# Moving weight conversion and erf, and adding idle-time products, in the first batch of a fused attention and feed-forward kernel

## Chip, cores and metric

The kernel runs on one core of one Trainium2 chip. The metric is the device time of one execution in microseconds (us). Every time below is a median over several executions of one build, all of them fast (one core, runs of one kernel within 1% of each other, with a mean granted clock of 0.976 or more; the granted clock is the share of TensorE's full clock that the profile shows). Times of single instructions come from one profiled execution of each kernel.

## The reference

Attention in both directions between a sequence `x` and a small `state`, and behind it a feed-forward block on all 4352 rows:

```python
B, H, S, Ns, D = 8, 8, 512, 32, 64          # d_model = H*D = 512, d_ff = 2048
scores  = scale * x @ state^T;  a  = softmax(scores);   xread = a  @ state     # (B,H,S,D)
scores2 = scale * state @ x^T;  a2 = softmax(scores2);  sread = a2 @ x         # (B,H,Ns,D)
rows = concat([xread, sread], axis=2)  ->  (B*(S+Ns), 512)                     # shortened
h  = rows @ w_in                       # 512 x 2048
g  = h * erf(softplus(h))
out = g @ w_out                        # 2048 x 512
```

`w_in` and `w_out` arrive as 64-bit floats. The kernel turns them into 32-bit floats itself, in eight pieces each.

## The kernel before

`xread @ w_in` is done as `a @ (state @ w_in)`: the code calls the inner product the *mixed* matrix (`m`), and each of the four *groups* of hidden columns of the first batch needs its own. A group g is: the mixed matrix, four hidden tiles (two products each, summed in one bank of PSUM, then *evicted*, that is read out of it, by ScalarE's softplus and VectorE's copy), erf and product, then 16 products with `w_out` (`project`). The mixed matrix of group g needs w_in pieces 2g and 2g+1; `project` of group g needs w_out pieces 2g and 2g+1. All of this shares three `raw` buffers for fetched pieces.

```python
def weight(dst, src, shape):
    ...
    raw = act.tile([P, 2 * shape[0] * i], U32, name="raw", bufs=3)
    fetched.append(nc.sync.dma_start(out=raw..., in_=src.bitcast(U32)))
    ...
    nc.scalar.activation(out=dst, in_=hi.bitcast(F32), func=ACTF.Copy, scale=2.0 ** -112)     # L111
    nc.scalar.activation(out=lo, in_=lo, func=ACTF.Copy, scale=2.0 ** -29)                     # L112
    nc.vector.tensor_scalar(d, d, 3, None, op0=ALU.logical_shift_left)                        # L113
    nc.vector.tensor_tensor(d, d, lo, op=ALU.add)                                             # L114
    nc.vector.scalar_tensor_tensor(out=d, in0=hi, scalar=0x80000000, in1=d, ...)              # L115
...
def warm(n):                      # idle-time products, for TensorE's clock (e1, e9)
    for _ in range(n):
        nc.tensor.matmul(out=spare[:, 0:P], lhsT=ident, rhs=ident, start=True, stop=True)
...
def hidden(b, fts, t0, n):
    ...
    for i in range(4):
        ...                                                        # products into hp
        banks.append((nc.scalar.activation(out=s[:, i, :], in_=hp, func=ACTF.Softplus),
                      nc.vector.tensor_copy(hs[:, i, :], hp)))
    nc.scalar.activation(out=s, in_=s, func=ACTF.Erf)
    return s, hs, nc.vector.tensor_tensor(s, s, hs, op=ALU.mult), banks
...
def weights(g, banks):            # first batch, after hidden() of group g
    if g + 1 < NG:
        for j in range(2):
            on_act, on_dve = banks[2 * j + 1]
            with tc.issue_after(on_act.ins), tc.issue_after(on_dve.ins):
                weights_in(2 * g + 2 + j)
        on_act, on_dve = mixed(0, g + 1)
    else:
        on_act, on_dve = banks[3]
    with tc.issue_after(on_act.ins), tc.issue_after(on_dve.ins):
        weights_out(g)
...
    before, gT = gT, first()      # first() is hidden(), before is the group ahead
    if b == 0:
        weights(g, gT[3])
    if b == 0 and g == 3:
        with tc.issue_after(before[2].ins):
            rest()                # the state's attention of batch 0: exp, transposes, a2T, sT
    if pending is not None:
        pending()                 # project() of the group ahead
```

`issue_after(x)` puts the next instructions behind `x` in the order of the program. That order is fixed when the kernel is built, by an estimate of when each instruction is ready.

## Time and profile before

| what | before |
|---|---|
| time, median (range) of 3 runs | 818.99 us (818.62 to 820.32) |
| span of the profiled run | 819.1 us |
| TensorE busy | 97% |
| mixed matrix of group 1 starts | 45.91 us |
| group 2 / group 3 starts (first hidden product) | 73.69 / 96.31 us |
| `project` of group 2 ends | 120.86 us |
| attention transposes of batch 2 start | 131.69 us |

A line of the timeline gives start, duration, engine, source line, operation, output<-inputs, shapes and how many records were joined; in brackets is the idle time before it and what ended that. A product of the hidden tiles or with w_out is two records, each 0.43 us at a granted clock of 1.00 and 0.86 us at 0.50, from start to start (the text calls the two full clock and half clock). The prediction shows the page's main rows, the chain through the large hole and the clock windows; these lines of TensorE's timeline before complete them. They show group 3 without a hole of note: the products with w_out of group 2 start at 101.38 and flow on among small work.

```profile
96.31 3.70 PE L273 MATMUL h<-aT,m 128*128 128x512 f32 x8
...
101.38 1.98 PE L283 MATMUL o<-w_out,s 128*128 128x512 f32 x4 [0.82 <-DVE w_out L115]
...
111.32 9.61 PE L283 MATMUL o<-w_out,s 128*128 128x512 f32 x22
```

### The profile page before, as it was taken

Reading aid. Unit: us, or ns where it says so; the run is one execution under the profiler, and the core shown is the slowest. Engines: PE = TensorE matmul, PEld = TensorE weight load, DVE = VectorE, ACT = ScalarE, POOL = GpSimd, SP = SyncE. Lnnn points to the kernel's source line nnn. Section 1 sums busy time; section 2 is a strip of 40 time slices with the busy share of each in tenths; the row PEclk is TensorE's granted clock in tenths of the full one; section 3 lists DMA queues with packets and bytes.
Section 4 is the critical chain, followed back from the end, with each engine's and each line's share of the span. In section 5 each row is a group of like instructions: output and inputs, shape, how many; then the busy total and the mean of one; then the engine's idle time right before and its main releaser. Section 6 shows DMA issues by size and latency. Waiting matters only on the chain.

```text
span 819.1 us, 10493 instructions
## 1 busy us (share of the span) xinstructions
PE 791.8 (97%) x4460; PEld 605.8 (74%) x4460; DVE 429.0 (52%) x626; ACT 369.4 (45%) x465; POOL 0.7 (0%) x6
## 2 busy tenths in 40 slices
PE   7779999999999999999999999999999999999997
PEld 5223344678888788878888788878887888888886
DVE  3577785457445554547453744555454745353431
ACT  5557754637333733345343733363334533333320
POOL 0000000000000000000000000000000000000000
PEclk9769999999999999999999999999999999999999
DMA  6354730201100020002000020000000000000000
GB/s 209 129 179 149 234 103 26 79 0 25 54 0 27 1 78 0 27 1 78 0 26 1 16 63 1 26 1 26 1 27 1 27 1 26 1 26 1 26 1 26
DMA packets 47414, 35.27 MB, mean 43 GB/s; under 512 B 36872, under 2 KB 36872, under 8 KB 47368
## 3 DMA queue, kind: packets, MB, share of 16 engines
q1 hardware_dynamic: 45256, 34.09, 13.4%
q10 hardware_dynamic: 2112, 0.52, 0.3%
q8 instruction: 35, 0.57, 0.3%
q14 instruction: 11, 0.09, 0.0%
HBM read 25.69 MB, written 8.91 MB: 42 GB/s over the span
## 4 chain that ended last, share of the span: by engine, by line
PE 89%; ACT 5%; DVE 3%; issue 2%; DMA 1%; SPq 0%; DVEq 0%
PE o L335 44%; PE h L273 30%; PE at L256 4%; PE o L283 4%; PE at L157 1%; PE at L198 1%; PE at L180 1%; PE at L227 1%; PE at L215 1%; ACT s L277 1%; ACT L275 1%; ACT L277 1%; DMA x<-in_x_dram 1%; DVE w_in L114 1%; ACT s L275 1%
## 5 line engine op out<-in xcount | busy, mean ns | idle before, releaser
L273 PE MATMUL h<-aT,m 128*128 128x256 f32 (+1 forms) x960 | 245.4, 403 | 1.0 <-ACT m L258 0.7
L273 PEld LDWEIGHTS h<-aT,m 128*128 128x128 f32 x960 | 179.1, 192 | 66.6 <-issue 35.6
L276 DVE COPY hs<-h 128x512 f32<-128x512 f32 x136 | 93.4, 689 | 187.6 <-ACT s L275 187.6
L275 ACT ACTIVATE s<-h 128x512 f32<-128x512 f32 x136 | 80.4, 597 | 166.9 <-PE h L273 166.6
L278 DVE TENSOR_TENSOR s<-s,hs 128x2048 f32<-128x2048 f32 x34 | 77.9, 2292 | 80.1 <-ACT s L277 80.1
L335 PE MATMUL o<-w_out,s 128*128 128x256 f32 x480 | 114.9, 380 | 1.6 <-DVE s L278 1.6
L335 PE MATMUL o<-raw,hs 128*128 128x256 f32 x480 | 115.5, 380 | 0.0
L335 PE MATMUL o<-w_out,hs 128*128 128x256 f32 x480 | 113.4, 379 | 0.0
L335 PEld LDWEIGHTS o<-w_out,s 128*128 128x128 f32 x480 | 90.2, 190 | 14.3 <-DVE s L278 2.5
L335 PEld LDWEIGHTS o<-w_out,hs 128*128 128x128 f32 x480 | 91.1, 190 | 12.3
L335 PEld LDWEIGHTS o<-raw,hs 128*128 128x128 f32 x480 | 90.3, 190 | 12.4
L258 ACT COPY m<-at 128x512 f32<-128x512 f32 (+1 forms) x33 | 18.9, 573 | 163.4 <-PE at L256 163.4
L277 ACT ACTIVATE s<-s 128x2048 f32<-128x2048 f32 x34 | 64.9, 1910 | 0.4
L283 PE MATMUL o<-w_out,s 128*128 128x512 f32 x128 | 59.2, 602 | 1.3 <-DVE w_out L115 1.3
L335 PE MATMUL o<-raw,s 128*128 128x256 f32 x240 | 56.7, 379 | 0.0
L275 ACT ACT_TABLE_LOAD x40 | 51.3, 1283 | 0.7
L258 DVE COPY m<-at 128x512 f32<-128x512 f32 (+1 forms) x33 | 22.2, 674 | 54.9 <-PE at L256 54.9
L256 PE MATMUL at<-w_in,stT 64*32 64x512 f32 (+1 forms) x528 | 40.1, 609 | 10.6 <-DVE w_in L115 10.1
L335 PEld LDWEIGHTS o<-raw,s 128*128 128x128 f32 x240 | 45.2, 190 | 5.9
L283 PEld LDWEIGHTS o<-w_out,s 128*128 128x128 f32 x128 | 23.0, 190 | 32.3 <-issue 29.7
L277 ACT ACT_TABLE_LOAD x34 | 43.6, 1283 | 0.6
L346 ACT COPY m<-o 128x256 f32<-128x256 f32 x15 | 5.6, 372 | 57.3 <-PE o L335 57.3
(71 smaller groups left out, 569.2 us busy)
## 6 DMA issues: line engine op xcount, KB each, us to landing
raw<-in_moe_w_in_dram SPq DMA_DIRECT2D x8, 1024.0 KB, 5.7
raw<-in_moe_w_out_dram SPq DMA_DIRECT2D x8, 1024.0 KB, 4.8
out_dram<-ot SPq DMA_DIRECT2D x32, 256.0 KB, 2.4
x<-in_x_dram SPq DMA_DIRECT2D x60, 128.0 KB, 2.8
x<-in_x_dram ACTq DMA_DIRECT2D x4, 128.0 KB, 4.0
out_dram<-ot SPq DMA_DIRECT2D x8, 64.0 KB, 1.7
st<-in_state_dram SPq DMA_DIRECT2D x8, 56.0 KB, 4.1
st<-in_state_dram SPq DMA_DIRECT2D x2, 32.0 KB
```

Of the source, the lines that this page charges most:

```text
L114: nc.vector.tensor_tensor(d, d, lo, op=ALU.add)
L157: nc.tensor.transpose(out=xp[:, P * c:P * c + P], in_=xt[:, c, 2 * i:2 * i + 2, :], identity=ident)
L180: on_pe = nc.tensor.transpose(out=s1[:, NI * c:NI * c + NI, :], in_=sc[:, e, P * c:P * c + P], identity=ident)
L256: nc.tensor.matmul(out=ps[e][q, :], lhsT=stT[b][r, q], rhs=w_in[r, fs, i, :], start=True, stop=True)
L258: return nc.scalar.copy(mg[:, 0], ps[0]), nc.vector.tensor_copy(mg[:, 1], ps[1])
L273: nc.tensor.matmul(out=hp[:, n * j:n * j + n], lhsT=lhsT, rhs=rhs, start=(k == 0), stop=(k == len(ops) - 1))
L275: banks.append((nc.scalar.activation(out=s[:, i, :], in_=hp, func=ACTF.Softplus), nc.vector.tensor_copy(hs[:, i, :], hp)))
L276: nc.vector.tensor_copy(hs[:, i, :], hp)))
L277: nc.scalar.activation(out=s, in_=s, func=ACTF.Erf)
L278: return s, hs, nc.vector.tensor_tensor(s, s, hs, op=ALU.mult), banks
L283: nc.tensor.matmul(out=acc[r], lhsT=gT[:, i, P * r:P * r + P], rhs=w_out[:, GF * g + i, :], start=(g == 0 and i == 0), stop=(g == NG - 1 a ...
L335: nc.tensor.matmul(out=acc[bank][:, E2 * c:E2 * c + E2], lhsT=lhs[:, i, :], rhs=rhs[:, g, i, :], start=(first and i == 0 and c == 0), stop ...
```

## The change

The intent is to let w_in be converted sooner, since TensorE sleeps for it in group 0, and to keep TensorE's granted clock at 1.00, which in before fell to 0.50 behind the first hole. Four parts: (1) 12 more idle-time products; (2) in group 0 the two next pieces of w_in are converted between the evictions of the tiles, not behind erf; (3) erf and product (`finish`) go behind the next mixed matrix; (4) the two w_out pieces of a group are converted between the evictions of the *next* group instead of right behind the mixed matrix.

```diff
-    def weights_out(g):
-        for t in range(GF * g, GF * g + GF, 2):
-            weight(w_out[:, t:t + 2, :], ...)
+    def weights_out(j):
+        weight(w_out[:, 2 * j:2 * j + 2, :], ...)
...
-        nc.scalar.activation(out=s, in_=s, func=ACTF.Erf)
-        return s, hs, nc.vector.tensor_tensor(s, s, hs, op=ALU.mult), banks
+
+        def finish():
+            nc.scalar.activation(out=s, in_=s, func=ACTF.Erf)
+            return nc.vector.tensor_tensor(s, s, hs, op=ALU.mult)
+        return s, hs, finish, banks
...
-            warm(20)
+            warm(32)
...
-    def weights(g, banks):
-        ...                                    # shown above
+    def behind(pair, f, *args):
+        with tc.issue_after(pair[0].ins), tc.issue_after(pair[1].ins):
+            return f(*args)
+
+    def weights(g, banks, finish):
+        for j in range(2):
+            if g > 0:
+                behind(banks[j], weights_out, 2 * g - 2 + j)
+            if g + 1 < NG:
+                behind(banks[3] if g else banks[j], weights_in, 2 * g + 2 + j)
+        at = mixed(0, g + 1) if g + 1 < NG else banks[3]
+        end = behind(at, finish)
+        if g + 1 == NG:
+            for j in range(2):
+                behind(at, weights_out, 2 * g + j)
+        return end
...
-            before, gT = gT, first()
+            gT = first()
             if b == 0:
-                weights(g, gT[3])
+                before, end = end, weights(g, gT[3], gT[2])
+            else:
+                gT[2]()
```

(The cuts are the unchanged arguments of `weight`, the matching line for `rest()` and the start value of `end`.)

More of the change, by code (lines that the diff above doesn't have):

```diff
@@ L123, in weights_in @@
                (NK, 2 * P))
-    def weights_out(g):
-        for t in range(GF * g, GF * g + GF, 2):
-            weight(w_out[:, t:t + 2, :],
-                   moe_w_out[P * t:P * t + 2 * P].rearrange("(t p) e -> p t e", p=P),
-                   (2, d_model))
+    def weights_out(j):
+        weight(w_out[:, 2 * j:2 * j + 2, :],
+               moe_w_out[2 * P * j:2 * P * j + 2 * P].rearrange("(t p) e -> p t e", p=P),
+               (2, d_model))
     spare = ps_o.tile([P, d_model], F32, name="o3")
@@ L420 @@
     mixed(0, 0, 2)
-    def weights(g, banks):
-        if g + 1 < NG:
-            for j in range(2):
-                on_act, on_dve = banks[2 * j + 1]
-                with tc.issue_after(on_act.ins), tc.issue_after(on_dve.ins):
-                    weights_in(2 * g + 2 + j)
-            on_act, on_dve = mixed(0, g + 1)
-        else:
-            on_act, on_dve = banks[3]
-        with tc.issue_after(on_act.ins), tc.issue_after(on_dve.ins):
-            weights_out(g)
-    pending = last = gT = None
+    def behind(pair, f, *args):
[10 more added lines that the diff above has]
+        if g + 1 == NG:
+            for j in range(2):
+                behind(at, weights_out, 2 * g + j)
+        return end
+    pending = last = end = None
     for b in range(B + 1):
@@ L451 @@
                 states(b + 1)
-            before, gT = gT, first()
+            gT = first()
             if b == 0:
-                weights(g, gT[3])
+                before, end = end, weights(g, gT[3], gT[2])
+            else:
+                gT[2]()
             if b == 0 and g == 3:
-                with tc.issue_after(before[2].ins):
+                with tc.issue_after(before.ins):
                     rest()
```

## The prediction

> **What bounds the kernel now.** I read the page first, then the chain of work that ended last, then the first 150 us of the timeline, then windows of 2 us for the granted clock.
>
> From the page:
>
> ```profile
> PE 791.8 (97%) x4460; PEld 605.8 (74%) x4460; DVE 429.0 (52%) x626; ACT 369.4 (45%) x465; POOL 0.7 (0%) x6
> ...
> PEclk9769999999999999999999999999999999999999
> ...
> L256 PE MATMUL at<-w_in,stT 64*32 64x512 f32 (+1 forms) x528 | 40.1, 609 | 10.6 <-DVE w_in L115 10.1
> ```
>
> TensorE is busy 97%, so only its holes and its slow stretches can be won. Of 27 us of holes, 10.1 are in one row: the matrix product (L256) that waits for a converted piece of w_in. The clock row has its only low digits in slices 2 to 4, 20 to 61 us. Both belong to the first batch, where weights are still fetched and converted. After it, nothing that the change touches is left: the last 436 of the program's order rows on TensorE are the same in both kernels. The effect is thus a constant shift, fixed near 147 us, when the second batch starts.
>
> The chain around the large hole:
>
> ```profile
> 36.78 1.04 ACT w_in L111
> 37.84 1.28 ACT L277
> 39.14 1.92 ACT s L277
> 41.14 2.15 issue
> 43.29 1.23 DVE w_in L114
> 44.54 1.24 DVE w_in L115
> 45.91 2.06 PE at L256 x16
> 48.59 6.50 PE h L273 x8
> ```
>
> The reader sees the erf (with its table) and the product ("issue") of group 0 standing between the first and last steps of the conversion of w_in piece 3 (pieces count from 0). TensorE ended group 0 at 36.15, sleeps 9.76 us, and then runs 8 records at 0.81 us instead of 0.43.
>
> The windows give the clock (third number from the end):
>
> ```profile
> 16.00:18.00 2.00, 1.98 (x18) 1.78 (x16) 2.00 (x5) 2.00 (x3) 0.00 (x0) 1.00 0.00 0
> 18.00:20.00 2.00, 0.00 (x0) 0.00 (x0) 1.99 (x5) 0.31 (x1) 0.00 (x0) 1.00 0.00 0
> 20.00:22.00 2.00, 1.29 (x6) 1.16 (x7) 1.58 (x4) 0.00 (x0) 0.00 (x0) 0.53 0.56 110
> 22.00:24.00 2.00, 1.69 (x12) 0.48 (x10) 2.00 (x4) 0.24 (x1) 0.00 (x0) 0.50 1.00 373
> ...
> 30.00:32.00 2.00, 2.00 (x19) 0.48 (x18) 0.69 (x2) 0.97 (x2) 0.00 (x0) 0.91 0.58 238
> ```
>
> A hole of 2.7 us (17.98 to 20.70) halves the clock from about 20.1 to 30.4, and the hole of 9.76 us halves it from about 40.6 to 54.2.
>
> Later groups are already dense. Group 2:
>
> ```profile
> 73.69 3.60 PE L273 MATMUL h<-aT,m 128*128 128x512 f32 x8
> ...
> 77.73 2.84 PE L283 MATMUL o<-w_out,s 128*128 128x512 f32 x6 [0.45 <-DVE w_out L115]
> ```
>
> Group 2 starts at 73.69 and group 3 at 96.31: a period of 22.6 us for 21.7 us of products (4 evicted tiles at 1.72, 16 w_out products at 0.86, one mixed matrix at 1.05). w_out is converted before the evictions, so it costs 0.45 us of waiting.
>
> [...]
>
> **The change part by part.** A conversion takes, start to start, on ScalarE 1.03 twice (L111, L112), on VectorE 0.6, 1.13 and 1.24 (L113 to L115). An eviction is 0.50 to 0.60 on ScalarE, 0.60 to 0.69 on VectorE; erf 1.9, table 1.28, product 2.2. Nearly nothing is added or removed; these move. I walked the new order of each queue with these durations[...].
>
> *Longer warm-up.* 12 more at 0.23 us: the idle-time products end at 20.76 instead of 17.98, just where the transposes start (20.70). The clock stays up: three hidden products of 1.72 us take 0.86. Tile 3 of group 0 ends at 31.7 instead of 36.15.
>
> *w_in pieces between evictions, erf and product behind.* ScalarE: softplus 1 ends at 28.6; L111, L112, L111, softplus 2, L112 run to 33.2. VectorE is then the limit: its L114 of piece 2 ends 31.9, L113 32.5, copy 33.1, L115 34.25, copy 34.85, L114 36.0, L115 37.27. The mixed matrix starts at 37.35, not 45.91: **8.56 won**. TensorE still sleeps 5.6 us, so the clock still falls.
>
> *Group 1.* Its first tile starts at 40.0 (was 48.59). erf and product now follow the copies: erf ends 43.1, product 45.4, the copy of tile 0 46.05. The four tiles end at 49.55. But w_out piece 0 now is converted behind softplus 1: softplus 46.1, L112 48.2, L114 49.45, then L113 and copy 2, L115 at 51.85. The first w_out product stalls from 49.55 to 51.9. 16 of them and the mixed matrix follow: group 2 starts at 66.75, not 73.69. **6.9 left.**
>
> *Group 2.* Tiles 66.75 to 73.65. Softplus 1 ends 70.85; wo L112 72.9; L114 74.15; L113 and copy 2 75.35; L115 76.5. TensorE stalls 2.9 us, where it lost 0.45. Group 3 starts at 76.55 + 13.8 + 1.05 = 91.4, not 96.31: **4.9 left**.
>
> *Group 3.* Here the new order of ScalarE is softplus 0 and 1, table, the two exp of the state's attention, table, softplus 2 and 3, a copy, and only then w_out. Softplus 3 ends near 101.05 (three tables); copy, L111, L112 103.7; L114, L115 106.2. TensorE has ended the tiles at 98.9 and has 1.6 us of attention work, so 5.7 us idle, and the clock falls. Before, the same products began at 101.38. Then three w_out products (5.2 us cold) and a wait for a ScalarE copy that stands behind erf and two more conversions, 111.5. The other 13 take 11.2 after the 64 small records: project 2 ends near 123.85, not 120.86. **3.0 lost.**
>
> *Into batch 2.* Four subtractions (2.2 each) that were spread now stand together in front of the mixed copies; they end at 127.5, and the third mixed matrix waits 0.8 us. One w_out product has moved to fill the hole of 0.44 at the second batch's transposes. The attention transposes start at 133.2 with one product fewer done (131.69 before), 1.5 + 0.86 - 0.44 = **1.9 us later**.
>
> Sum: -8.6 + 1.6 + 2.0 + 7.9 - 1.0 = +1.9, so about 820.9. Hence the intent works where the chain shows it, and is given back where w_out moves behind evictions that TensorE needs less urgently than w_out itself.
>
> **The rivals.** (1) The gain survives. If the real order of landing lets w_out be ready when tile 3 ends, the stalls of groups 1 and 2 vanish and 812 to 815 result. For it: 8.6 us at 37 us are solid, and before had only 0.45 of such a stall. Against it: L115 of the piece is four VectorE steps behind softplus 1, and the tiles need only 3.4 us after tile 1. (2) The clock falls in the stalls of groups 1 and 2 too. [...] (3) The clock is not held at 20 us[...]: 2.5 us less won, 823. (4) A transfer binds: w_in pieces now reuse the buffers of w_out pieces. Piece 7 can be fetched only from 76.5, lands 4.7 later by the page's landing times, and its conversion ends at 86.0, just when the mixed matrix is due. It is hidden, with no slack; 1 to 2 us worse otherwise.
>
> **Range and chances.** 821.0, since (2) and (3) add a little and (1) takes as much. My walk has some 30 steps with errors of 0.1[...]: 815 to 825.5. 2% is 16.4 us. The whole first-batch hole with its cold clock is some 13 us, so faster by 2% is out of reach; slower would need several falls of the clock at once. Faster 0.02, same 0.96, slower 0.02.
>
> **What would show it.** Right: L256 of group 1 at about 37.4; clock 1.0 through 20 to 37; w_out product stalls of 2 to 3 us in groups 1 and 2, released by DVE w_out L115; TensorE nearly idle from 99 to 106; second batch 1 to 3 us later than before. Wrong: no such stalls, or a period of group 2 below 23 us (then rival 1); low clock near 75 to 82 us (rival 2) or 20 to 27 us (rival 3). The whole number fails if the group 3 hole is much shorter than 5 us, for it alone decides the sign.

The sum: -8.6 + 1.6 + 2.0 + 7.9 - 1.0 = +1.9 us on 819.0, so 820.9. The walk took a step to start when the step ahead of it on its engine and its inputs were done; that was the assumption. What it took from the trace of before is measured: a table load is 1283 ns and an erf 1910 (the L277 rows of the page), ScalarE idled 0.6 us in all ahead of the 34 loads for erf and 0.4 us ahead of the 34 erf, and VectorE's copy of a hidden tile waited for ScalarE's softplus, 187.6 us in all (the L276 row). "Cold" in the recorded texts stands for stretches with a granted clock of 0.50.

## The result and the profile after

| | before | after |
|---|---|---|
| time, median (range) of 4 runs | 819.65 us (818.62 to 821.04) | 826.61 us (825.56 to 827.86) |
| span of the profiled run | 819.1 us | 824.5 us |

The ratio of after to before is 1.0084, with a 95% interval of 1.0062 to 1.0107: slower by 6.9 us, inside the 2% that counts as the same. A ratio here is the mean time of one kernel's fast runs over that of the other's of the same rounds, so it is not quite the ratio of the medians. The two profiled spans differ by 5.4 us; both reach the first idle-time products of the attention at the same 13.35 us. Most of the other 1.5 us comes from which executions were profiled: before's profile is of an execution of 820.84 us, 1.2 above its median, and after's of one of 826.34, 0.3 below. Before's 29 timed runs beside the experiments sort by their mean granted clock: 819.7 us on average at 0.987 (15 runs), 820.7 at 0.985 (12, the profile's value too) and 822.2 at 0.983 (2). After's four runs don't: the one with the highest clock, 0.991, took 826.87 us.

Source lines of after are one or two off those of before: L272 is before's L273 (hidden product), L255 its L256 (mixed), L285 its L283 (w_out), L278 its L277 (erf). In e5, e8 and e10 to e12 these are one higher, and in e6 w_out is L282.

From the page of after: the clock row, the two TensorE rows with the most idle time ahead of them (last column), and the median landing time of a weight piece (last number, us). Behind them stand the same two landing rows from the page of before.

```profile
PEclk9899989999999999999999999999999999999999
...
L285 PE MATMUL o<-w_out,s 128*128 128x512 f32 x128 | 62.0, 630 | 9.3 <-DVE w_out L115 9.3
...
L255 PE MATMUL at<-w_in,stT 64*32 64x512 f32 (+1 forms) x528 | 39.1, 602 | 6.9 <-DVE w_in L115 6.1
...
raw<-in_moe_w_in_dram SPq DMA_DIRECT2D x8, 1024.0 KB, 6.6
raw<-in_moe_w_out_dram SPq DMA_DIRECT2D x8, 1024.0 KB, 5.9
```

```profile
raw<-in_moe_w_in_dram SPq DMA_DIRECT2D x8, 1024.0 KB, 5.7
raw<-in_moe_w_out_dram SPq DMA_DIRECT2D x8, 1024.0 KB, 4.8
```

The wait for w_in fell from 10.1 us to 6.1, and a wait for w_out grew from 1.3 us (the w_out row of before's page) to 9.3. Counted from 1, slices of the clock row are better in after at 2 and 3 (8 and 9, in before 7 and 6) and worse at 6 (8 for 9), which is group 3: the windows show half clock from about 106.4 to 113.2 us. A shorter fall in group 2 doesn't show in the row. The timeline of TensorE after tells where the time goes:

```profile
37.79 1.96 PE L255 MATMUL at<-w_in,stT 64*32 64x512 f32 x16 [5.53 <-DVE w_in L115]
...
52.75 9.71 PE L285 MATMUL o<-w_out,s 128*128 128x512 f32 x22 [2.43 <-DVE w_out L115]
62.98 1.09 PE L255 MATMUL at<-w_in,stT 64*32 64x512 f32 x16 [0.52 <-DVE w_in L115]
...
68.40 7.03 PE L272 MATMUL h<-aT,m 128*128 128x512 f32 x16
78.36 11.40 PE L285 MATMUL o<-w_out,s 128*128 128x512 f32 x22 [2.94 <-DVE w_out L115]
...
95.11 1.02 PE L272 MATMUL h<-aT,m 128*128 128x512 f32 x2
...
105.22 0.65 PE L226 MATMUL at<-x,a2T 128*32 128x64 f32 x32 [1.41 <-ACT a2T L216]
109.80 4.52 PE L285 MATMUL o<-w_out,s 128*128 128x512 f32 x6 [3.93 <-DVE w_out L115]
```

Read it as a ledger against before. The mixed matrix of group 1 comes 8.1 us earlier (37.79 for 45.91). Two stalls for w_out, 2.43 and 2.94 us, eat into that. The 22 records behind the second stall take 11.40 us, where 22 records behind the first take 9.71. Group 3 starts only 1.2 us ahead of before (95.11 for 96.31). In it TensorE is nearly idle for 6 us and starts the products with w_out at 109.80, before at 101.38.

The windows of 2 us show the clock after (third number from the end): full at 20 to 24 us, where before had 0.53 and 0.50, and 0.50 just behind group 2's stall (from 79.1 to 82.5 us).

```profile
20.00:22.00 2.00, 1.69 (x14) 1.31 (x13) 1.97 (x5) 0.00 (x0) 0.00 (x0) 1.00 0.48 102
22.00:24.00 2.00, 1.51 (x20) 0.46 (x18) 2.00 (x4) 1.12 (x2) 0.00 (x0) 1.00 0.99 376
...
78.00:80.00 2.00, 1.64 (x3) 0.82 (x4) 2.00 (x4) 1.80 (x2) 0.00 (x0) 0.77 0.22 58
80.00:82.00 2.00, 2.00 (x3) 0.66 (x2) 2.00 (x3) 0.00 (x0) 0.00 (x0) 0.50 0.88 276
```

Last, ScalarE's timeline after: it waits for two pieces of w_in that were asked for late, because their buffer was held by a piece of w_out (the DMA queue waits for DVE w_out L115 four times from 20 to 120 us, 52.0 us in all). They were issued at 52.76 and 78.37 (from the DMA queue's timeline), so they took 5.35 and 5.79 us from issue to use.

```profile
58.11 1.15 ACT L111 ACTIVATE w_in<-raw 128x1024 f32<-128x1024 f32 x1 [3.92 <-DMA raw<-in_moe_w_in_dram]
...
84.16 1.14 ACT L111 ACTIVATE w_in<-raw 128x1024 f32<-128x1024 f32 x1 [4.36 <-DMA raw<-in_moe_w_in_dram]
```

### The profile page after: what moved, and what is told of

Read it like the earlier page. It is cut to its first block, busy times and chain, and to the rows that moved or that the text cites. A ratio compares the mean times of both kernels' runs of the same rounds, so it can differ in the third digit from the quotient of the medians.

```text
span 824.5 us, 10544 instructions
## 1 busy us (share of the span) xinstructions
PE 793.4 (96%) x4484; PEld 607.9 (74%) x4484; DVE 429.7 (52%) x626; ACT 370.2 (45%) x466; POOL 0.7 (0%) x6
## 4 chain that ended last, share of the span: by engine, by line
PE 88%; ACT 6%; DVE 3%; DMA 1%; issue 1%; SPq 0%
PE o L337 44%; PE h L272 28%; PE o L285 6%; PE at L255 4%; PE at L156 1%; ACT raw L112 1%; PE at L179 1%; PE at L226 1%; ACT L274 1%; ACT s L274 1%; PE at L197 1%; PE at L214 1%; ACT w_out L111 1%; DMA raw<-in_moe_w_in_dram 1%; DMA x<-in_x_dram 1%
## 5 line engine op out<-in xcount | busy, mean ns | idle before, releaser
L272 PE MATMUL h<-aT,m 128*128 128x256 f32 (+1 forms) x960 | 242.3, 400 | 1.6 <-DVE hs L275 0.9
L272 PEld LDWEIGHTS h<-aT,m 128*128 128x128 f32 x960 | 178.0, 191 | 65.9 <-issue 32.6
L337 PEld LDWEIGHTS o<-w_out,hs 128*128 128x128 f32 x480 | 91.2, 190 | 12.3
L285 PE MATMUL o<-w_out,s 128*128 128x512 f32 x128 | 62.0, 630 | 9.3 <-DVE w_out L115 9.3
L278 ACT ACTIVATE s<-s 128x2048 f32<-128x2048 f32 x34 | 64.9, 1910 | 0.4
L285 PEld LDWEIGHTS o<-w_out,s 128*128 128x128 f32 x128 | 24.2, 199 | 42.5 <-issue 30.8
L274 ACT ACT_TABLE_LOAD x41 | 52.6, 1283 | 0.7
L255 PE MATMUL at<-w_in,stT 64*32 64x512 f32 (+1 forms) x528 | 39.1, 602 | 6.9 <-DVE w_in L115 6.1
L278 ACT ACT_TABLE_LOAD x34 | 43.6, 1283 | 0.6
```

The costliest lines, as they stand in the source:

```text
L255: nc.tensor.matmul(out=ps[e][q, :], lhsT=stT[b][r, q], rhs=w_in[r, fs, i, :], start=True, stop=True)
L272: nc.tensor.matmul(out=hp[:, n * j:n * j + n], lhsT=lhsT, rhs=rhs, start=(k == 0), stop=(k == len(ops) - 1))
L285: nc.tensor.matmul(out=acc[r], lhsT=gT[:, i, P * r:P * r + P], rhs=w_out[:, GF * g + i, :], start=(g == 0 and i == 0), stop=(g == NG - 1 a ...
L337: nc.tensor.matmul(out=acc[bank][:, E2 * c:E2 * c + E2], lhsT=lhs[:, i, :], rhs=rhs[:, g, i, :], start=(first and i == 0 and c == 0), stop ...
```

## The experiments

Twelve kernels were run, each beside before in the same rounds; all gave correct results. Before's median was 819.61, 820.41 and 820.45 us in the three sets. The theory: parts 1 to 3 win in group 0, and part 4 (w_out behind the next evictions) gives that back through stalls and, most of all, in group 3. The rivals: the deferred erf costs the time; the half clock in group 2 costs it; late pieces of w_in cost it.

One caution for single profiles: the first piece of `x` lands at different times, so the idle-time products start anywhere from 12.73 to 14.58 us in the 14 profiles. Absolute times of two profiles can differ by as much; where it matters, the text says so. The start of group 3 is a fair mark to compare by: in before, after, e2, e4, e5 and e6 TensorE has run the same 64 records with w_out by then.

| run | kernel | median us | ratio to before (95%) |
|---|---|---|---|
| after | the change | 826.61 | 1.0084 (1.0062 to 1.0107) |
| e1 | before, longer warm-up | 816.93 | 0.9956 (0.9941 to 0.9971) |
| e9 | after, short warm-up | 830.82 | 1.0124 (1.0110 to 1.0138) |
| e4 | new order in group 0 only | 814.57 | 0.9934 (0.9918 to 0.9949) |
| e6 | before, w_out a group later | 837.46 | 1.0194 (1.0168 to 1.0219) |
| e2 | after, erf not deferred | 829.41 | 1.0111 (1.0093 to 1.0129) |
| e5 | after, clock held in the stalls | 827.63 | 1.0086 (1.0073 to 1.0099) |
| e3 | after, w_out piece 4 earlier | 827.35 | 1.0082 (1.0065 to 1.0100) |
| e7 | after, state's attention earlier | 820.63 | 1.0001 (0.9988 to 1.0014) |
| e8 | combination | 810.12 | 0.9871 (0.9856 to 0.9887) |
| e10 | e4 with products in the hole | 813.52 | 0.9916 (0.9903 to 0.9930) |
| e11 | e8, w_out 0 and 1 between evictions | 811.87 | 0.9899 (0.9886 to 0.9913) |
| e12 | e8 without products in the hole | 814.42 | 0.9928 (0.9915 to 0.9942) |

### e1 and e9: the warm-up alone

e1 is before with one number changed, e9 is after with it changed back.

```diff
-            warm(20)
+            warm(32)          # e1, in before; e9 is the reverse, in after
```

> The kernel before with 32 instead of 20 idle-time products, nothing else. Theory (the hole at 18 to 20.7 us halves the clock and delays group 0, and the delay is carried on): clock 1.0 from 20 to 36 us, group 0 ends near 31.8 instead of 36.15, the mixed matrix of group 1 starts near 41.5 instead of 45.9, and the time falls by 3.5 to 4.5 us against the kernel before. Rival (the conversions on ScalarE and VectorE set the pace of the first batch whatever the clock does): group 0 ends earlier, but the mixed matrix moves less than 1 us and the time less than 1 us.

Measured: 0.9956 of before, 3.6 us less. The hole for w_in stays (9.75 us in e1's trace), as it must.

> The changed kernel with 20 idle-time products as before, nothing else undone: what the longer warm-up is worth inside the change. Theory (its 12 products keep the clock up for group 0, and what group 0 gains is carried through the conversions): half clock from 20 to 30 us, group 0's tiles and the mixed matrix of group 1 about 3.5 to 4 us later (41.5 instead of 37.8), the time 3 to 4.5 us above the changed kernel (829.5 to 831). Rival (later waits absorb it): less than 1.5 us.

Measured: 1.0124, against 1.0084 for after, so 3.3 us more. In its trace the clock is 0.50 at 22 to 24 and 26 to 28 us, and the mixed matrix of group 1 starts at 40.49 instead of 37.79. Both directions agree: part 1 is worth 3 to 4 us, and through the transposes and small products directly behind the longer idle-time products the clock stayed at 1.00 (20 to 24 us of after). The rival of the prediction that doubted this falls.

### e4: the new order in group 0 alone

After's warm-up and group 0 are kept; in groups 1 and 2 erf, w_in and (from group 1 on) w_out go back to where before has them. Only w_out pieces 0 and 1 still stand between the evictions of group 1.

```diff
+        if g:
+            end = finish()
         for j in range(2):
-            if g > 0:
-                behind(banks[j], weights_out, 2 * g - 2 + j)
+            if g == 1:
+                behind(banks[j], weights_out, j)
             if g + 1 < NG:
-                behind(banks[3] if g else banks[j], weights_in, 2 * g + 2 + j)
+                behind(banks[2 * j + 1] if g else banks[j], weights_in, 2 * g + 2 + j)
         at = mixed(0, g + 1) if g + 1 < NG else banks[3]
-        end = behind(at, finish)
-        if g + 1 == NG:
+        if g == 0:
+            end = behind(at, finish)
+        else:
             for j in range(2):
                 behind(at, weights_out, 2 * g + j)
```

> The new order in group 0 alone (w_in pieces 2 and 3 between its evictions, its erf and product behind the next mixed matrix, longer idle-time products); w_out of group 0 behind group 1's evictions; from then on everything as in the kernel before, so w_out of groups 1 and 2 is converted ahead of the next evictions. Theory (the early gain of 8 us is real, and only w_out behind later evictions gives it back): mixed matrix of group 1 near 37.8, group 2 starts near 67.5 instead of 73.7, groups 2 and 3 keep the period of 22.6 us, and the time is 5 to 7 us below the kernel before, 813 to 815. Rival (total conversion work bounds the first batch, so what is won at the start is lost in group 1, which has six pieces to convert): group 2 starts no earlier than 71, and the time is within 2 us of the kernel before.

Measured: 0.9934, 5.4 us less than before and 1.5%, or 12.3 us, less than after. So what after does from group 1 on costs 12 us, more than the whole of what it wins. This run undoes the deferred erf, the place of w_in and the place of w_out together; e6 and e2 take two of them singly. In e4's trace group 2 runs without a stall and group 3 starts 22.1 us after it (90.37 and 68.24), where after needs 26.7 (95.11 and 68.40):

```profile
68.24 3.60 PE L272 MATMUL h<-aT,m 128*128 128x512 f32 x8
71.68 1.88 PE L285 MATMUL o<-w_out,s 128*128 128x512 f32 x4
...
90.37 2.74 PE L272 MATMUL h<-aT,m 128*128 128x512 f32 x6
```

It also shows a limit: beyond e1's warm-up, the new order of group 0 won only 0.2% (0.9956 to 0.9934); group 1 still waited 1.81 and 1.15 us for the w_out pieces left between its evictions.

### e6: w_out late, alone, in before

Before with part 4 only (`weights_out` is rewritten as in the change, which is cut here).

```diff
+        if g > 0:
+            for j in range(2):
+                with tc.issue_after(banks[j][0].ins), tc.issue_after(banks[j][1].ins):
+                    weights_out(2 * g - 2 + j)
         if g + 1 < NG:
             ...
-        with tc.issue_after(on_act.ins), tc.issue_after(on_dve.ins):
-            weights_out(g)
+        if g + 1 == NG:
+            for j in range(2):
+                with tc.issue_after(on_act.ins), tc.issue_after(on_dve.ins):
+                    weights_out(2 * g + j)
```

> The kernel before with one part of the change alone: w_out of group g is converted between the evictions of group g+1 instead of ahead of them. Short warm-up, w_in pieces and erf as before. Theory (this part is what gives the gain back): groups 1 and 2 each stall 2.5 to 3 us for DVE w_out L115, group 3 idles 5 us and more, and the time rises by 8 to 12 us over the kernel before, to 828 to 832. Rival (it hurts only together with the deferred erf and product): the time rises by less than 3 us.

Measured: 1.0194, 15.9 us more (the run that spreads most, 832.77 to 838.48). The direction was expected, the size not. Group 3 starts at 103.30, in before at 96.31, so 7.0 us are lost ahead of it: two stalls of 2.94 us, and slow products behind each (26 records in 12.89 us and 28 in 13.98, 0.50 us each, where 22 in before took 9.61, 0.44 each). In group 3 the program's order now puts all products of group 2 behind the state's attention and nine products of the mixed matrices, and these wait for the copy into the state's row block (`sT`):

```profile
119.49 2.39 PE L255 MATMUL at<-w_in,stT 64*32 64x512 f32 x10 [5.00 <-ACT sT L234]
122.44 16.69 PE L282 MATMUL o<-w_out,s 128*128 128x512 f32 x32 [0.57 <-DVE w_out L115]
```

Part 4 alone is enough to make the kernel slower. What lies behind the start of group 3 comes with a different order there, which after doesn't have.

### e2: is it the deferred erf?

```diff
+        end = finish()
         for j in range(2):
             ...
-        end = behind(at, finish)
```

> The changed kernel, but erf and product of a group are asked for at once again, not behind the next mixed matrix; the scheduler then places them after the last piece's ScalarE half. Theory (w_out's place gives the gain back, the place of erf matters little): mixed matrix of group 1 still near 37.8 us, the w_out stalls of groups 1 and 2 stay at 2 to 3 us, the time within 2 us of the changed kernel. But the program's order here puts 9 of 16 w_out products of group 2 wholly behind the attention work of group 3, so up to 3 us more are possible. Rival (the deferred erf is what costs): the wait of TensorE for evictions in groups 1 to 3 goes and 4 us or more come back.

Measured: 1.0111, against 1.0084: 2.2 us slower than after. The stalls for w_out stay (2.92 us in both groups), so erf behind the mixed matrix doesn't make them. This run too got e6's order in group 3, with a wait of 4.99 us for `sT`, so its time cannot price the deferral. But ahead of that order it gained nothing either: group 3 starts at 96.50, in after at 95.11. That rules out that undoing the deferral recovers the loss.

### e5: is it the half clock?

Eleven idle-time products (22 records) fill the stalls of groups 1 and 2. (Here and in e8 and e10 to e12 the lines that record `last_mm` in `hidden()` are cut.)

```diff
+    def hold(n):
+        ps = ps_at.tile([P, P], F32, name="at")
+        with tc.issue_after(last_mm[0].ins):         # last hidden product of the group
+            for _ in range(n):
+                nc.tensor.matmul(out=ps, lhsT=ident, rhs=ident, start=True, stop=True)
+
     def weights(g, banks, finish):
+        if g in (1, 2):
+            hold(11)
```

> The changed kernel with 11 more idle-time products (2.55 us) after the last hidden product of group 1 and of group 2, into a spare bank, where TensorE otherwise waits 2.4 and 2.9 us for the first w_out piece. Theory (the wait in group 2 lets the clock fall, which cost 1.7 us in the 22 w_out records, 11.40 us instead of 9.71): clock 1.0 from 70 to 100 us, those records take 9.7 us; but the mixed matrix behind them then waits for w_in piece 7, whose transfer could start only at 78.4 and whose conversion ended at 88.9, so only 0.7 to 1.2 us of the 1.7 are had: the time falls by about 1 us. First rival (the clock alone): the whole 1.7 us. Second rival (clock irrelevant): nothing.

Measured: 1.0086, no gain, where about 1 us was expected. The clock was held (1.00 in each window from 76 to 84 us) and the 20 records after the stall took 9.19 us, but the next mixed matrix then waited for w_in, and started at 89.42, where after had 89.70:

```profile
78.75 9.19 PE L286 MATMUL o<-w_out,s 128*128 128x512 f32 x20 [0.47 <-DVE w_out L115]
...
89.42 1.09 PE L256 MATMUL at<-w_in,stT 64*32 64x512 f32 x16 [1.49 <-DVE w_in L115]
```

Two costs overlap here: the half clock, and the late transfer of w_in piece 7, which was issued at 78.75 and used from 84.55, 5.80 us later. Taking one away shows the other, but they are not of one size. In after, piece 7 was converted 0.8 us before the mixed matrix began (89.70):

```profile
87.65 1.23 DVE L115 SCALAR_TENSOR_TENSOR w_in<-raw,w_in 128x1024 uint32<-128x1024 uint32 x1
```

So there the products slowed by the half clock (0.50 from 79.1 to 82.5 us) were what held the mixed matrix up, and at full clock it could have begun 0.8 us earlier at most, when the piece was ready. In e5, the build also put one product less ahead of the mixed matrix (20 records for 22, 0.86 us), which is part of its 1.49 us of waiting. Group 3 starts at 95.7 (after: 95.11), so nothing was gained by then; behind it the clock was at half for 10.2 us, in after for 6.8, so the time of the whole run is not a clean price of the clock. A kernel with a fourth `raw` buffer, meant to let the transfer start earlier, does not build, so there is no run of it and that side is left open.

### e3: only w_out piece 4 earlier

```diff
-            if g > 0:
+            if g > 0 and (g, j) != (3, 0):
                 behind(banks[j], weights_out, 2 * g - 2 + j)
...
         end = behind(at, finish)
+        if g == 2:
+            behind(at, weights_out, 4)
```

> The changed kernel, but w_out piece 4 (first half of group 2's) is converted behind the mixed matrix of group 3, ahead of group 3's evictions; all else as changed. Theory (TensorE idles from 99 to 110 us for piece 4 alone): the waits of 3.9 and 1.4 us before the first w_out product of group 2 go; some of it comes back as a wait for the state copies that now stand behind pieces 5 and 6, about 3 us; project 2 ends 3 to 6 us earlier and the time falls by 3 to 6 us against the changed kernel, to about 821 to 823. Rival (VectorE is full there, so moving one piece only moves the hole): the evictions of group 3 come later by the 2 us and the time moves by less than 1.5 us.

Measured: 1.0082, no gain. The products of group 2 do start at 104.19 instead of 109.80 (and e3's profile runs 1.1 us late from its start), but a hole of 4.50 us appears behind them:

```profile
104.19 1.02 PE L285 MATMUL o<-w_out,s 128*128 128x512 f32 x2
...
116.60 1.91 PE L226 MATMUL at<-x,a2T 128*32 128x64 f32 x64 [4.50 <-ACT a2T L216]
```

ScalarE's copies for the state's attention (`a2T`) now stand, at 115.97 us, behind erf (110.04) and the halves of two conversions (111.86 to 116.09). The rival reading, that the hole only moves, was right, though it blamed VectorE: in this trace ScalarE's queue in group 3 is the limit, not one piece of w_out. (The build also parted the two exponentials: ScalarE has six table loads of 1.28 us between 92 and 110 us, in after five between 91 and 109.)

### e7: the state's attention out of group 3

```diff
-            if b == 0 and g == 3:
+            if b == 0 and g == 2:
                 with tc.issue_after(before.ins):
                     rest()
```

> The changed kernel with the state half of the first batch's attention (two exp with their table, two copies, some small work) asked for one group earlier, in group 2. Theory (in group 3 ScalarE's queue is too full: evictions, exp with two table loads, erf and 8 conversion halves stand ahead of what TensorE waits for): the idle time of TensorE in group 3 falls from 6.6 us (waits of 1.4, 3.9, 0.8 and 0.4) to below 3; some 2 us are lost in group 2 instead; the time falls by 2 to 5 us against the changed kernel. Rival (the place of w_out pieces 4 and 5 behind all evictions makes the hole by itself): the time moves by less than 1 us.

Measured: 1.0001, against 1.0084 for after: 6 to 7 us less, somewhat more than was expected. The exponentials, copies and table loads of the state leave ScalarE's queue (they run at 79.20 to 82.02 and 93.96 to 97.52 us) before w_out pieces 4 and 5 need it (from 104.52). Group 3 starts later (97.49) and its products with w_out start no earlier: w_out piece 4 is ready at 110.4 us, in after at 109.8 (12.9 us behind the start of the group instead of 14.7). But TensorE does the state's work and two mixed matrices ahead of them (busy 11.4 of the 14 us from 97 to 111, in after 8.3; the clock row of e7's page shows 9 in slices 5 and 6, where after's mean from 97 to 111 us is 0.84), and then they run without a break:

```profile
97.49 3.60 PE L272 MATMUL h<-aT,m 128*128 128x512 f32 x8
...
110.43 14.00 PE L285 MATMUL o<-w_out,s 128*128 128x512 f32 x32 [1.61 <-DVE w_out L115]
```

They end at 124.4 us, after's at 127.2. The loss in group 3 thus hangs on where the state's attention stands, and is of the same size as the whole slowdown. How much of it is ScalarE's queue, and how much that TensorE had its other work earlier and no half clock there, this run doesn't part.

### e8, e10, e11, e12: the parts that win, combined

e8 keeps the warm-up and w_in between the evictions of group 0, does erf at once, converts w_out piece 0 behind the last eviction of group 0, piece 1 behind the first eviction of group 1 and the others where before had them, and fills the hole of group 0 with 23 products.

```diff
+        end = finish()
+        if g == 0:
+            with tc.issue_after(last_mm[0].ins):
+                warm(23)
         for j in range(2):
-            if g > 0:
-                behind(banks[j], weights_out, 2 * g - 2 + j)
+            if g == 1 and j == 1:
+                behind(banks[0], weights_out, 1)
             if g + 1 < NG:
-                behind(banks[3] if g else banks[j], weights_in, 2 * g + 2 + j)
+                behind(banks[2 * j + 1] if g else banks[j], weights_in, 2 * g + 2 + j)
+        if g == 0:
+            behind(banks[3], weights_out, 0)
         at = mixed(0, g + 1) if g + 1 < NG else banks[3]
-        end = behind(at, finish)
-        if g + 1 == NG:
+        if g:
             for j in range(2):
                 behind(at, weights_out, 2 * g + j)
```

> A version meant to beat both. The new order in group 0 alone as in the fourth run, but its erf and product at once (ScalarE is idle then), w_out piece 0 converted right behind group 0's evictions while TensorE waits for w_in piece 3, piece 1 between group 1's evictions, 23 idle-time products in that hole to hold the clock; groups 2 and 3 as in the kernel before. Theory (TensorE's stalls in group 1 are waits for w_out pieces and a cold clock, both of which this fills): mixed matrix near 38.5, no wait over 1 us for w_out in group 1, group 2 starts near 64 to 65 instead of 68.2 in the fourth run, time 809.5 to 812. Rival (VectorE is full from 30 to 65 us, and work pulled forward delays the copies that TensorE needs): group 2 starts no earlier than 67, time 813.5 to 816.

Measured: 810.12 us, 0.9871: the fastest of all, 10.5 us ahead of before. Its clock row shows 9 throughout, and group 2 starts at 62.93 where before had 73.69:

```profile
PEclk9999999999999999999999999999999999999999
```

```profile
38.12 1.09 PE L256 MATMUL at<-w_in,stT 64*32 64x512 f32 x16 [0.88 <-DVE w_in L115]
...
62.93 3.60 PE L273 MATMUL h<-aT,m 128*128 128x512 f32 x8
```

The other three take e8 apart. e10 is e4 with the 23 products in the hole.

```diff
         if g:
             end = finish()
+        else:
+            with tc.issue_after(last_mm[0].ins):
+                warm(23)
```

> The fourth run (new order in group 0 alone) with 23 more idle-time products in the 5.5 us in which TensorE waits for w_in piece 3, nothing else. Theory (with erf and product deferred behind the mixed matrix, the evictions of group 1 wait for them and not for TensorE): clock 1.0 throughout, the first 8 hidden records take 3.6 us instead of 5.3, but the third tile waits for VectorE's copy until about 46 us as before, so the time stays within 1 us of the fourth run. Rival (the cold clock itself costs): 2 to 3 us less than the fourth run, about 812.

Measured: 0.9916 against 0.9934 for e4. Holding the clock is worth 1 to 1.5 us there: the first eight hidden records run in 3.70 us instead of 5.31, but then TensorE waits 2.45 us for VectorE's copy (`hs`), where e4 waited 0.84, and behind that wait the clock falls after all (1.00 from 44 to 48 us, 0.57 from 48 to 52): the next eight records take 5.40 us instead of 3.70. Again one limit hid another.

e11 puts w_out pieces 0 and 1 back between the evictions of group 1.

```diff
-            if g == 1 and j == 1:
-                behind(banks[0], weights_out, 1)
+            if g == 1:
+                behind(banks[j], weights_out, j)
...
-        if g == 0:
-            behind(banks[3], weights_out, 0)
```

> The combined version (eighth run) but w_out pieces 0 and 1 both between group 1's evictions, as in the change; erf at once, clock held. Theory (a w_out piece placed behind softplus 1 comes 5.5 us after it, TensorE needs it 3.5 us after): one wait of 2 to 3 us for DVE w_out L115 in group 1, group 2 starts near 65 to 66, time 811.5 to 813.5. Rival (holding the clock and an early erf make all of the gain): within 0.7 us of the eighth run, 810.

Measured: 0.9899, 2.3 us more than e8. The stall of after is back, with everything else in e8's order:

```profile
49.41 7.13 PE L286 MATMUL o<-w_out,s 128*128 128x512 f32 x16 [2.94 <-DVE w_out L115]
```

e12 takes the 23 products out of e8.

```diff
-        if g == 0:
-            with tc.issue_after(last_mm[0].ins):
-                warm(23)
```

> The combined version (eighth run) without the 23 idle-time products in the hole. Theory (there TensorE and its clock set the pace in group 1, nothing else): half clock from about 36 to 45 us, the mixed matrix takes 1.96 instead of 1.09 us and the hidden records of group 1 some 2 us more; the time is 2 to 3.5 us above the eighth run, 812 to 813.5. Rival (the cold clock is hidden behind conversions, as it was in the changed kernel's group 2): within 0.7 us.

Measured: 0.9928, 4.7 us more than e8 and above what was expected. Not all of it is clock (0.59, 0.50 and 0.63 in the three windows of 4 us from 36 to 48 us): without these products the build ordered the first w_out product ahead of the hidden tiles of group 1, where it waited 2.88 us. How the two share the 4.7 us is open.

## Why the prediction was right and where it was wrong

The prediction said 821.0 us, 815 to 825.5, within 2%. It was within 2%, but at 826.6 it lies 1.1 us above the range. Its own steps against the trace:

| step | before | predicted | measured |
|---|---|---|---|
| mixed matrix of group 1 starts | 45.91 | 37.35 | 37.79 |
| first w_out product of group 1 behind the stall | | 51.9 | 52.75 |
| group 2 starts | 73.69 | 66.75 | 68.40 |
| stall for w_out in group 2 | 0.45 | 2.9 | 2.94 |
| group 3 starts | 96.31 | 91.4 | 95.11 |
| w_out products in group 3 start | 101.38 | 106.25 | 109.80 |
| `project` of group 2 ends | 120.86 | 123.85 | 127.18 |
| shift of the second batch | | +1.9 | +5.4 |

**Right.** The warm-up: the clock held (1.00 from 20 to 24 us), confirmed by e1 and e9 (3.6 and 3.3 us). The 8.6 us at the first hole (8.1 measured). The stalls for w_out in groups 1 and 2, their length and their releaser (DVE w_out L115); e11 brings the group 1 stall back by part 4's order alone. The loss in group 3: predicted +7.9 from group 3's start to the end of its `project` against before; measured 127.18 - 95.11 = 32.07, before 120.86 - 96.31 = 24.55, so +7.5. e7 ties it to the state's attention in that group; that ScalarE's order is the whole of it is argued from the queue. That this hole "alone decides the sign" fits: with the state moved (e7), the kernel was level with before.

**Wrong: "group 3 starts at 76.55 + 13.8 + 1.05 = 91.4" (step of group 2).** This is the step that failed. The prediction took 13.8 us for the 16 w_out products behind the stall and 1.05 for the mixed matrix, at full clock. Measured was 16.75 us for the same stretch (95.11 - 78.36), 1.9 more. This is the largest term of the 3.5 us that the sum missed in the profiled runs. The prediction had it as rival 2 and left it out of the middle estimate on the ground that rival 1 would take as much; the fall came in group 2 (0.5 from 79.1 to 82.5 us; 22 records in 11.40 us, 9.71 at full clock) and rival 1 did not come at all. Why one stall is followed by half clock and another is not, these runs don't show. In after the stall of 2.43 us in group 1 was not (1.00 from 50 to 60 us); in e2 and e6 stalls of 2.9 us in both groups were each followed by slow products (26 to 28 records, 0.50 us each), and so was that of 2.92 us in group 1 of e9 (22 records in 11.19 us); in e11 one of 2.94 us was not (1.00 from 44 to 52 us, 16 records in 7.13 us).

**Wrong: "lands 4.7 later by the page's landing times".** The page of before has 5.7 us for pieces of w_in and 4.8 for those of w_out, so the working took about the figure of the wrong row. The pieces of w_in concerned took 5.35 and 5.79 us. The first cost 0.52 us of waiting at 62.98, where none was predicted, and is part of group 2's start at +1.65 against the prediction. The second was not waited for in after, because the half clock had already made the mixed matrix late; e5 took the half clock away and met it (1.49 us of waiting). With the piece ready at 88.88 and the mixed matrix begun at 89.70, 0.8 us of the group 2 loss was the clock's alone; the rest (an estimate: 1.9 - 0.8 = 1.1 us) would have stayed at full clock. The prediction weighed each of the two as if the other were absent.

**Small terms.** The low digits of the clock row are slices 2 and 3 (20.5 to 61.4 us), not "2 to 4"; nothing rests on it. The walk was 0.44 us early at the first mixed matrix and 0.41 more at the w_out of group 1. After group 3's start it was 0.4 us too slow. Together, from the table: 0.44 + 0.41 + 0.80 (rest of group 1, with the 0.52) + 0.16 (group 2's tiles) + 1.90 - 0.38 = 3.3 us up to the end of `project`; some 0.2 us more came on the way into the second batch.

**Not settled.** Means differ by 6.9 us, the profiled spans by 5.4; the profile of before is of one of its slower executions, and why executions of one kernel differ in clock isn't in a trace. Whether piece 7 took longer than piece 5 because the loads of the state and of `x` were issued right behind it (from 78.79 us) was not tried: moving those loads also moved TensorE's work in group 3. And of after's part from group 1 on, w_in behind the last eviction was never undone by itself.

## What to carry to other kernels

With ScalarE's queue full, moving a conversion ahead of one consumer put another behind it here (e3: the products with w_out 5.6 us earlier, and then a hole of 4.50 us for `a2T`): before moving one, ask for both consumers how soon they need it, and put first the piece whose consumer comes first. A half clock, a late transfer and a wait on a queue lay on top of each other here, so that removing one won little (e5 nothing, e10 1 to 1.5 us); test removals in pairs before calling one of them harmless. And look at the last place where the queues are mixed (here group 3 with the state's attention), since a gain made earlier can be lost there: after was 1.2 us ahead of before at the start of group 3 and 6.3 us behind at the end of its `project` (127.18 for 120.86).
